# An attention and MLP kernel: the last row tile of the output in column parts of 384 and 128

## The chip, the cores and the metric

The kernel runs on one core of a Trainium2 chip. The metric is the device time of one execution in microseconds. The core has TensorE (PE) for matmuls, with a queue of weight loads of its own (PEld), VectorE (DVE), ScalarE (ACT), GpSimd (POOL) and SyncE (SP), which issues DMA transfers here. PE writes its results to PSUM, in tiles of 128 partitions by up to 512 f32 columns.

## The reference

Two things are computed one after the other. First, attention with a choice of key chunks, for 4 batches, 8 heads, 768 positions and a head size of 64; then a layer norm and a two-layer MLP with a residual, over rows of 512 (8 heads by 64):

```python
# attention, per batch and head: 24 chunks of 32 keys, 6 chosen for each query
ub = sum(max(q * k_min, q * k_max), -1)          # per query and chunk
top_chunks = argsort(where(causal, ub, -1e9))[..., -6:]
scores = q @ k.T / sqrt(64)
attn = softmax(where(chosen & causal, scores, -1e9))
x = (attn @ v)                                    # -> [4, 768, 512]
# MLP
xn = (x - mean) / sqrt(var + 1e-6) * g_ln
out = x + maximum(xn @ w_ch1, 0) @ w_ch2          # w_ch1 [512, 2048], w_ch2 [2048, 512]
```

## The kernel before

A unit of attention is `g`: one batch and one pair of heads, 16 in all. A half `r` is three row tiles of 128 positions (`TR` = 3), so a batch has two halves. For a unit, `load_qk` and `load_v` fetch its inputs, `turn` transposes them on PE, `k_bound` (DVE) and `k_copy` (ACT) read the transposed keys from one PSUM tile `tr`, `q_copy`, `q_ring` and `mask_ring` fill operand buffers, `bounds` and `select` choose the chunks, `scores` computes scores and their exponentials, `diag` (POOL) clears what lies above the diagonal, and `values` and `normalise` make `x`.

For a half of a batch, `stats`, `centre`, `x_t` and `rstd` do the norm. `mlp1(b, r, m)` computes two of the 16 blocks of the hidden layer: 8 matmuls of 384 columns (line 512) and one ReLU on ACT into `hT` (line 516). `mlp2(b, r, i, j)` computes a quarter of the contraction for row tile `i`: four matmuls of 512 columns (line 524) that add to one PSUM tile `yp`. After the quarter `j` = 3, DVE scales `yp` by `rstd` and adds `x` into `ot` (line 530), and SP stores `ot` (line 535). The `ot` pool has two buffers.

`w1_load` and `w2_load` fetch the weights in quarters, on POOL's queue, as `load_v` does; each w2 quarter holds the rows that one `j` needs.

The order of the program is written as a list of 894 pieces. A piece is one call of such a function, and it has a time, in units of one `g`, at which it should come. A table `MOVED` adds an offset to the time of a piece or of all pieces with the same first arguments (the longest matching key counts). The sorted list is the order in which the pieces are written. The pieces of the first part (`begin`, up to the norm of batch 0) are tied together in that order on each of PE, DVE, ACT and POOL. The others are placed by a scheduler that takes the list's order as priority, on each engine's queue, and it may let a ready piece go ahead of one that it thinks is waiting. Semaphores for all of it, PSUM tiles included, are made by the framework.

The last pieces of the list before the change are `mlp2(3, 1, 2, j)`, for the third row tile of the last half, in the order j = 0, 2, 1, 3.

Of the kernel before, what the change touches and what calls it, by code (L numbers as in the profile page):

```python
# [19 lines left out]
def kernel(  # L20
# [13 lines left out]
    nc = tc.nc  # L34
    P = nc.NUM_PARTITIONS

    B, H, S, D = q.shape
# [4 lines left out]
    NR = 2  # L42
    TR = NT // NR
# [4 lines left out]
    DM = H * D  # L48
    HID = moe_w_ch1.shape[1]
    KT1 = DM // P  # L50
    KT2 = HID // P
# [98 lines left out]
    w2b = const.tile([P, KT2, DM], F16, name="w2b", tag="w2b")  # L150
# [21 lines left out]
    def xh(b, r):  # L172
        if (b, r) not in x_tiles:
            x_tiles[b, r] = xp.tile([P, TR, H, D], F32, name="x", tag="x")
        return x_tiles[b, r]
# [215 lines left out]
    for r in range(NR):  # L391
        n = 0
# [125 lines left out]
    def mlp2(b, r, i, j):  # L518
        h = hf[b, r]
        if j == 0:  # L520
            h["yp"] = ps_t.tile([P, DM], F32, name="yp", tag="one")
        yp = h["yp"]
        for kt in range(4 * j, 4 * j + 4):
            nc.tensor.matmul(  # L524
                yp, h["hT"][:, kt, i * P:(i + 1) * P], w2b[:, kt, :],
                start=(kt == 0), stop=(kt == KT2 - 1),
            )
        if j == 3:
            ot = outp.tile([P, DM], F32, name="ot", tag="ot")
            nc.vector.scalar_tensor_tensor(  # L530
                ot, yp, h["rstd"][:, i:i + 1], xh(b, r)[:, i].rearrange("p h d -> p (h d)"),
                op0=ALU.mult, op1=ALU.add,
            )
            s = TR * r + i
            nc.sync.dma_start(out[b, s * P:(s + 1) * P, :], ot)
# [34 lines left out]
    for n in range(-3, U + LAG + 1):  # L570
# [13 lines left out]
        if new:  # L584
            g, i = new
# [76 lines left out]
    for b in range(B):  # L662
        e = 4.0 * b + GAP
        for r in range(NR):
            f = e + (-0.56 if r == 0 else 0.0)
            if b > 0:
                for i in range(TR):
                    at(f, stats, b, r, i)
                for i in range(TR):
                    at(f, centre, b, r, i)  # L670
                for kt in range(KT1):
                    at(f + 0.01, x_t, b, r, kt)
            at(f + 0.2 if b > 0 else ready[r], rstd, b, r)
        e += 0.06
        z = 4.0 * (b + 1) + GAP + 0.06
        m = (e + z) / 2
        if b == 0:
            spread(mlp1, b, 0, ready[0], -1.0)
            spread(mlp2, b, 0, -1.0, e)
            spread(mlp1, b, 1, e, m)  # L680
            spread(mlp2, b, 1, m, z)
            continue
        spread(mlp1, b, 0, e, m)
        spread(mlp1, b, 1, m, z)
        spread(mlp2, b, 0, m + 0.01, z)
        spread(mlp2, b, 1, z + 0.01, z + 2.0)
# [5 lines left out]
            (2,): 0, (2, 4): 0.006, (2, 5): 0.028, (3,): 0, (3, 1): 0.013, (3, 2): 0.013,  # L692
            (4,): -0.048, (5,): 0.008, (5, 5): 0.016, (6,): 0.004, (7,): -0.067, (7, 1): -0.07,
            (8,): -0.436, (9,): -0.025, (9, 5): -0.02, (11,): -0.044, (12,): -0.311, (13,): -0.144,
            (14,): -0.138, (14, 5): -0.134, (15,): -0.21, (15, 4): -0.176, (15, 5): 0,
        },
        "centre": {
            (): 0.008, (0,): -0.017, (0, 1): 0, (0, 1, 0): -0.017, (1,): 0, (1, 0, 2): 0.089,
            (1, 1): 0.033, (1, 1, 1): 0.026,
# [3 lines left out]
            (3, 0): -0.003, (3, 1): 0, (4,): -0.056, (6, 0): -0.044, (6, 1): -0.066, (7, 0): -0.178,  # L703
            (7, 1): -0.097, (8, 0): -0.399, (8, 1): -0.6, (9, 0): -0.066, (9, 1): -0.069, (11, 0): 0,
            (11, 1): -0.054, (12, 0): -0.04, (12, 1): 0, (13, 0): -0.146, (13, 1): -0.078,
            (14, 0): 0.003, (14, 1): 0, (15, 0): -0.621,
# [8 lines left out]
            (0,): -0.004, (1, 0): 0.161, (1, 1): 0.063, (2,): 0.006, (3, 0): -0.011, (3, 1): 0.054,  # L715
            (4,): 0.024, (5, 0): 0.511, (5, 1): 0.42, (6,): 0.038, (7, 0): -0.032, (9, 1): 0.023,
            (10,): 0.034, (11, 1): 0.026, (12, 0): 0.938, (12, 1): 0.253, (13, 0): 0.002,
            (13, 1): 0.073, (14,): 0.046, (15,): 0.034,
        },
        "k_diag": {  # L720
            (1,): 0.041, (2, 0): 0.13, (3, 0): 0.033, (3, 1): 0.01, (4,): -0.002, (6,): 0.002,
# [12 lines left out]
            (2,): -0.087, (3, 0): -0.13, (3, 1): -0.568, (4,): -0.551, (5,): -0.547, (6,): -0.163,  # L734
            (7,): 0.215, (8,): -0.124, (9,): 0.342, (12,): 0.279, (13,): 0.241, (14,): 0.301,
            (15,): 0.238,
        },
        "mask_ring": {
            (): 0.017, (0, 0): 0.021, (0, 1): 0, (1, 0): 0.036, (1, 1): -0.009, (2, 0): 0.023,
            (2, 1): 0, (4,): 0.064, (5,): 0.074, (6,): 0.076, (7,): 0.016, (8,): -0.257, (9,): 0.076,  # L740
# [5 lines left out]
            (13,): -0.082, (14,): 0, (15,): -0.006,  # L746
        },
        "mlp1": {
            (0, 0, 2): -0.016, (0, 0, 6): 0.106, (0, 0, 10): 0.098, (0, 0, 14): 0.069,
            (0, 1): -0.023, (0, 1, 0): 0, (0, 1, 2): 0.016, (0, 1, 14): 0.055, (1,): -0.026,  # L750
            (1, 0, 0): 0.016, (1, 0, 2): 0.016, (1, 0, 4): 0.028, (1, 0, 8): -0.014,
            (1, 1, 0): -0.036, (1, 1, 4): -0.178, (1, 1, 10): 0, (1, 1, 14): -0.001, (2,): -0.294,
            (2, 0, 6): -0.616, (2, 0, 12): -0.277, (2, 1, 2): -0.353, (2, 1, 6): -0.28,
            (2, 1, 10): -0.228, (3,): 0.103, (3, 0, 2): 0, (3, 0, 4): 0, (3, 0, 12): 0,
            (3, 0, 14): 0, (3, 1, 0): 0, (3, 1, 4): 0.108, (3, 1, 6): 0, (3, 1, 14): 0.094,
        },
        "mlp2": {
            (): -0.156, (0, 0, 1, 0): -0.071, (0, 0, 1, 3): 0, (0, 0, 2, 0): -0.051, (0, 1): -0.154,
# [5 lines left out]
            (2, 0, 2, 3): -0.34, (2, 1): 0, (2, 1, 0, 0): -0.34, (2, 1, 0, 1): -0.18,  # L764
            (2, 1, 0, 2): -0.323, (2, 1, 0, 3): -0.298, (2, 1, 1, 0): -0.267, (2, 1, 1, 1): -0.298,
            (2, 1, 1, 2): -0.423, (2, 1, 1, 3): -0.568, (3,): -0.233, (3, 0, 0): 0,
            (3, 0, 0, 2): -0.124, (3, 0, 0, 3): -0.233, (3, 0, 2): -0.332, (3, 1, 0, 0): -0.332,
            (3, 1, 0, 1): -0.374, (3, 1, 1, 1): -0.263, (3, 1, 1, 2): -0.443, (3, 1, 1, 3): -0.009,
            (3, 1, 2, 0): -0.009, (3, 1, 2, 1): 0.115, (3, 1, 2, 2): -0.224, (3, 1, 2, 3): -0.152,
        },  # L770
        "normalise": {
            (1, 0): -0.008, (2,): 0.002, (3,): -0.004, (4, 0): -0.01, (4, 1): -0.002, (6,): 0.002,
            (7,): -0.058, (8,): -0.331, (9,): 0.002, (12,): 0.006, (13,): -0.032, (14, 0): 0.065,
            (14, 1): 0.028,
# [4 lines left out]
            (11,): -0.002, (12, 0): 0, (12, 1): 0.16, (13,): -0.026, (14, 0): 0.066, (14, 1): 0.028,  # L779
        },  # L780
        "q_copy": {
            (): 0.051, (0,): 0.005, (1, 0): 0.005, (1, 1): 0, (2, 0): 0.007, (2, 1): 0, (3,): -0.012,
# [6 lines left out]
            (11,): 0.063, (12,): -0.045, (13,): 0.022,  # L789
# [3 lines left out]
            (10,): 0.167, (11,): 0, (12,): 0.141, (13,): 0.114, (14,): 0.096,  # L793
# [5 lines left out]
            (0,): -0.015, (0, 0, 0): -0.007, (0, 0, 1): 0.015, (1,): 0.018, (1, 1): 0.002,  # L799
            (1, 1, 2): 0.059, (1, 1, 3): 0.047, (2,): 0.038, (2, 1): 0.023, (2, 1, 0): -0.014,  # L800
            (2, 1, 1): 0.021, (3,): 0.017, (3, 0): 0.016, (4,): 0.001, (4, 1, 3): 0, (5, 1): -0.013,
            (5, 1, 0): 0, (6,): -0.144, (6, 1, 1): -0.087, (6, 1, 2): -0.133, (6, 1, 3): -0.092,
            (7,): -0.134, (7, 0, 0): -0.079, (7, 1, 0): -0.114, (7, 1, 2): -0.18, (8,): -0.582,
            (8, 0, 0): -0.504, (8, 0, 1): -0.612, (9,): -0.011, (9, 1): 0.013, (9, 1, 0): -0.011,
            (10,): -0.013, (10, 1, 2): -0.017, (10, 1, 3): -0.017, (11, 0, 0): 0.047,
            (11, 0, 1): 0.051, (11, 1, 0): -0.103, (11, 1, 1): -0.006, (11, 1, 2): 0.113,
            (11, 1, 3): 0.065, (12, 1, 2): -0.128, (12, 1, 3): -0.007, (13,): -0.028,
            (13, 0, 0): -0.042, (13, 1, 2): -0.062, (13, 1, 3): -0.042, (14,): 0.015,
            (14, 1, 3): 0.138, (15,): -0.31, (15, 1, 0): -0.355,
        },  # L810
        "select": {
            (1, 1): 0.01, (2, 0): -0.003, (2, 1): 0.002, (3, 0): -0.004, (3, 1): 0.048, (4,): 0.059,
            (5,): 0.335, (6,): 0.013, (7,): -0.056, (8,): -0.234, (9,): 0.454, (11,): -0.008,
            (12,): 0.17, (13,): -0.024, (14,): 0.028, (15,): 0.025,
# [19 lines left out]
            (): 0.027, (2,): 0.029, (3,): 0,  # L834
        },
        "x_t": {
            (): 0.474, (0,): 0.003, (0, 0, 0): 0, (0, 0, 3): 0.004, (0, 1, 1): -0.012,
            (1, 0, 0): 0.324, (2,): 0.123, (2, 0, 3): 0.242, (2, 1): 0.24, (2, 1, 3): 0.286,
            (3,): 0.695, (3, 1, 2): 0.739, (3, 1, 3): 0.529,
# [12 lines left out]
    for _, _, fn, args, kept in sorted(pieces, key=lambda x: x[:2]):  # L852
        done = nc.cur_bb.bb.instructions
        n = len(done)
# [36 lines left out]
```

## Time and profile before

| | |
|---|---|
| median of 7 runs | 303.09 us (302.03 to 303.98) |
| the profiled execution, its own time | 303.68 us |
| its span in the profile | 301.4 us |
| TensorE clock granted, mean | 0.999 |
| matmuls (PE) busy | 288.3 us |
| line 524, second MLP layer | 384 matmuls, 95.9 us busy, 379 ns each |
| line 530, the add on DVE | 24, 17.9 us, 745 ns each |
| line 535, stores of the output | 24 of 256 KB, median 2.2 us from issue to landing |

The span is the time from the first to the last instruction of the profile; the execution's own time is longer by what lies around it. In a row of a group, the numbers after the bar are the busy time in microseconds and the mean duration of one instruction in nanoseconds, then the idle time of the engine just before and what ended it. Matmuls are pipelined: their durations overlap, so the distance between the starts of two matmuls is what a sum needs. In the timeline the columns are start, length, engine, line, operation, and in brackets the idle time before it.

### The profile page before, as it was taken

What the parts mean: (1) busy time and instruction counts of PE and PEld (TensorE: products, weight loads), DVE (VectorE), ACT (ScalarE), POOL (GpSimd) and SP (SyncE); (2) the same over time, 40 slices, a digit from 0 to 9 for tenths busy, and PEclk for the clock granted to TensorE, in tenths of its full rate; (3) what the DMA queues carried; (4) which work ended last, traced back from release to release, by engine and by line L of the source; (5) the groups of instructions that cost most, each with busy time, mean ns of one, the idle gap of its engine ahead of it and who ended that gap; (6) DMA issues with size and microseconds to landing.
All of it is one profiled execution on the core that took longest, in us unless ns stands there. A gap on an engine that the chain in (4) does not pass through costs nothing.

```text
span 301.4 us, 7194 instructions
## 1 busy us (share of the span) xinstructions
PE 288.3 (96%) x2753; PEld 195.7 (65%) x2753; DVE 190.9 (63%) x654; ACT 183.4 (61%) x274; POOL 91.2 (30%) x162
## 2 busy tenths in 40 slices
PE   7887998999999999999999999999999999999993
PEld 3874766765777676777767667666666555555541
DVE  7888655679998788999577768577262282011011
ACT  3983998664788667778665674848368524423310
POOL 9559383152444412733230411223021120000000
PEclk9999999999999999999999999999999999999999
DMA  7999999999659659579482210113010110010111
GB/s 131 210 201 211 180 193 196 163 200 187 165 127 178 124 84 165 106 143 151 88 133 61 77 47 2 41 49 90 35 37 0 37 37 35 35 37 35 70 37 71
DMA packets 90226, 31.41 MB, mean 104 GB/s; under 512 B 78416, under 2 KB 87120, under 8 KB 90192
## 3 DMA queue, kind: packets, MB, share of 16 engines
q1 hardware_dynamic: 60416, 23.61, 34.2%
q0 software_dynamic: 29248, 7.34, 24.9%
q8 instruction: 22, 0.36, 0.5%
q14 instruction: 12, 0.10, 0.1%
q10 hardware_dynamic: 528, 0.00, 0.1%
HBM read 27.27 MB, written 6.29 MB: 111 GB/s over the span
## 4 chain that ended last, share of the span: by engine, by line
PE 75%; DMA 8%; POOL 7%; issue 4%; DVE 4%; ACT 1%; POOLq 0%; ACTq 0%
PE yp L524 24%; PE mm L512 24%; PE mm L411 10%; PE sm L437 6%; PE tr L223 4%; DMA w2b<-in_moe_w_ch_dram 4%; DMA w1b<-in_moe_w_ch_dram 4%; PE ub L326 3%; POOL va L214 2%; PE trh L497 1%; POOL pt L424 1%; PE trh L354 1%; DVE xc L482 1%; ACT pt L417 1%; POOL rstd L491 1%
## 5 line engine op out<-in xcount | busy, mean ns | idle before, releaser
L417 ACT ACTIVATE pt<-mm 128x1024 f16<-128x1024 f32 (+1 forms) x96 | 86.2, 918 | 25.7 <-PE mm L411 25.3
L524 PE MATMUL yp<-w2b,hT 128*128 128x512 f16 x384 | 95.9, 379 | 1.5 <-DMA w2b<-in_moe_w_ch_dram 1.5
L512 PE MATMUL mm<-xT,w1b 128*128 128x384 f16 x512 | 94.3, 326 | 0.0
L516 ACT ACTIVATE hT<-mm 128x768 f16<-128x768 f32 x64 | 51.9, 813 | 49.1 <-PE mm L512 48.8
L512 PEld LDWEIGHTS <-w1b 128*128 128x128 f16 x512 | 48.9, 98 | 29.9 <-issue 0.2
L524 PEld LDWEIGHTS <-hT 128*128 128x128 f16 x384 | 36.3, 98 | 31.8
L424 POOL TENSOR_SCALAR_AFFINE_SELECT pt<-pt 128x768 f16<-128x768 f16 x32 | 28.8, 899 | 89.2 <-ACT pt L417 89.2
L530 DVE SCALAR_TENSOR_TENSOR ot<-yp,rstd,x 128x512 f32<-128x512 f32 x24 | 17.9, 745 | 46.0 <-PE yp L524 46.0
L411 PE MATMUL mm<-QA,KA 128*128 128x128 f16 (+2 forms) x224 | 34.5, 245 | 1.0 <-ACT hT L516 0.5
L411 PE MATMUL mm<-QB,KB 128*128 128x128 f16 (+2 forms) x224 | 34.2, 246 | 0.0
L437 PEld LDWEIGHTS <-pt 128*128 128x128 f16 x672 | 24.6, 98 | 5.6 <-POOL pt L424 1.8
L437 PE MATMUL sm<-va,pt 128*128 128x65 f16 x672 | 26.5, 193 | 1.4 <-POOL pt L424 1.3
L411 PEld LDWEIGHTS <-KA 128*128 128x128 f16 x224 | 17.9, 99 | 8.1 <-issue 2.3
L471 DVE BATCH_NORM_STATS2 bst<-x 128x6 f32<-128x128 f32 x96 | 21.9, 281 | 0.8
L268 DVE TENSOR_REDUCE kc<-tr 128x12 f32<-128x384 f32 x32 | 17.5, 548 | 6.6 <-PE tr L223 4.9
L411 PEld LDWEIGHTS <-KB 128*128 128x128 f16 x224 | 17.9, 98 | 3.5 <-issue 0.8
L446 DVE RECIPROCAL rden<-sm 128x6 f32<-128x6 f32 x32 | 6.1, 191 | 19.7 <-PE sm L437 19.5
L447 DVE TENSOR_TENSOR x<-sm,rden 128x384 f32<-128x384 f32 x32 | 17.8, 556 | 1.0
L269 DVE TENSOR_REDUCE kc<-tr 128x12 f32<-128x384 f32 x32 | 17.5, 546 | 0.0
L223 PE MATMUL tr<-ident_f,qn 128*128 128x128 f32 x96 | 16.4, 281 | 1.0 <-DMA qn<-in_q_dram 0.8
L279 ACT CAST kh<-tr 128x384 f16<-128x384 f32 x24 | 11.6, 484 | 9.2 <-DVE kc L269 5.0
L223 PE MATMUL tr<-ident_f,kn 128*128 128x128 f32 x96 | 16.5, 283 | 0.0
(87 smaller groups left out, 354.6 us busy)
## 6 DMA issues: line engine op xcount, KB each, us to landing
kn<-in_k_dram SPq DMA_DIRECT2D x64, 96.0 KB, 3.4
qn<-in_q_dram SPq DMA_DIRECT2D x64, 96.0 KB, 3.8
out_dram<-ot SPq DMA_DIRECT2D x24, 256.0 KB, 2.2
va<-in_v_dram POOLq DMA_DIRECT2D x12, 192.0 KB, 5.8
w1b<-in_moe_w_ch_dram POOLq DMA_DIRECT2D x4, 512.0 KB, 8.2
w2b<-in_moe_w_ch_dram POOLq DMA_DIRECT2D x4, 512.0 KB, 11.1
KA<-kh SPq DMA_DIRECT2D x24, 48.0 KB, 2.4
KB<-kh SPq DMA_DIRECT2D x24, 48.0 KB, 2.0
```

What stands on the lines that cost most here:

```text
L223: nc.tensor.transpose(pst[:, t * P:(t + 1) * P], src[:, t], ident_f)
L268: nc.vector.tensor_reduce(kc[:, 0, n], view, axis=AX.X, op=ALU.min)
L411: nc.tensor.matmul(sc[:, hh, o:o + w * P], ks[:, t * P:(t + 1) * P], qs[:, s * P:(s + w) * P], start=True, stop=True,)
L417: nc.scalar.activation(pt[:, n0:n1].rearrange("p n h x -> p h n x"), sc[:, :, 0:o].rearrange("p h (n x) -> p h n x", x=P), ACTF.Exp, scale ...
L424: nc.gpsimd.affine_select(out=dv, in_=dv, compare_op=ALU.is_ge, fill=0.0, base=0, pattern=[[0, 2 * TR], [1, P]], channel_multiplier=-1,)
L437: nc.tensor.matmul(pv[:, hh, s2, :], pt[:, where[t, s], hh, :], va[:, hh, t, 0:D + 1], start=(t == 0), stop=(t == s),)
L447: nc.vector.tensor_tensor(xh(b, r)[:, :, 2 * hp:2 * hp + 2, :].rearrange("p s h d -> p h s d"), pv[:, :, :, 0:D], rden.to_broadcast([P, 2, ...
L471: nc.vector.bn_stats(h["st"][:, i, hp], xh(b, r)[:, i, 2 * hp:2 * hp + 2].rearrange("p h d -> p (h d)"),)
L512: nc.tensor.matmul(hp_[:, i, 0:TR * P], w1b[:, kt, (m + i) * P:(m + i + 1) * P], h["xT"][:, kt], start=(kt == 0), stop=(kt == KT1 - 1),)
L516: nc.scalar.activation(h["hT"][:, m:m + 2], hp_[:, :, 0:TR * P], ACTF.Relu, scale=HS)
L524: nc.tensor.matmul(yp, h["hT"][:, kt, i * P:(i + 1) * P], w2b[:, kt, :], start=(kt == 0), stop=(kt == KT2 - 1),)
L530: nc.vector.scalar_tensor_tensor(ot, yp, h["rstd"][:, i:i + 1], xh(b, r)[:, i].rearrange("p h d -> p (h d)"), op0=ALU.mult, op1=ALU.add,)
```

## The change

The last row tile of the output (batch 3, half 1, tile 2) is computed in two column parts. Its pieces j = 0 and 1 multiply the whole contraction, eight steps each, for columns 0 to 383; j = 2 and 3 do the same for columns 384 to 511. Each part is added and stored after its own last matmul, into a new `ot` buffer. Both parts use the one PSUM tile `yp`. All other row tiles are computed as before.

In the table, 66 pieces that had an offset of zero get one, and the four pieces of this row tile, which had offsets, have none, so that their order is 0, 1, 2, 3. All other offsets stay.

```diff
-        for kt in range(4 * j, 4 * j + 4):
+
+        n, cs = 4, slice(0, DM)
+        if (b, r, i) == (B - 1, NR - 1, TR - 1):
+            n, cs = 8, slice(0, DM - P) if j < 2 else slice(DM - P, DM)
+        for kt in range(n * j % KT2, n * j % KT2 + n):
             nc.tensor.matmul(
-                yp, h["hT"][:, kt, i * P:(i + 1) * P], w2b[:, kt, :],
+                yp[:, cs], h["hT"][:, kt, i * P:(i + 1) * P], w2b[:, kt, cs],
                 start=(kt == 0), stop=(kt == KT2 - 1),
             )
-        if j == 3:
+        if kt == KT2 - 1:
             ot = outp.tile([P, DM], F32, name="ot", tag="ot")
             nc.vector.scalar_tensor_tensor(
-                ot, yp, h["rstd"][:, i:i + 1], xh(b, r)[:, i].rearrange("p h d -> p (h d)"),
+                ot[:, cs], yp[:, cs], h["rstd"][:, i:i + 1], xh(b, r)[:, i].rearrange("p h d -> p (h d)")[:, cs],
                 op0=ALU.mult, op1=ALU.add,
             )
             s = TR * r + i
-            nc.sync.dma_start(out[b, s * P:(s + 1) * P, :], ot)
+            nc.sync.dma_start(out[b, s * P:(s + 1) * P, cs], ot[:, cs])
```

In the table, the pieces whose place in time changes most are these (offset in units of one `g`, before and after):

| piece | before | after |
|---|---|---|
| load_v(0, 0), (1, 0), (1, 1) | 0 | -0.126 |
| load_v(0, 1) | 0 | -0.08 |
| w1_load(3, 3) | 0 | 0.023 |
| w2_load(0, 0), (1, 0), (2, 1), (3, 1) | 0 | 0.047, 0.035, -0.032, -0.038 |
| k_diag(2, 1); mask_ring(2, 1) | 0 | 0.13; 0.136 |
| mlp2(0, 0, 1, 3) | 0 | -0.156 |
| k_copy(8, 0), (8, 1) | 0 | -0.141, -0.216 |
| load_v(10), (11) | 0 | 0.5, 0.265 |
| q_ring(11) | 0 | 1.082 |
| pair_stats(12, 0) | 0 | 0.16 |
| diag(12, 1) | 0 | -0.108 |
| bounds(15, 5) | 0 | -0.21 |
| mlp1(3, 0, 2), (3, 0, 4), (3, 0, 12), (3, 0, 14), (3, 1, 0) | 0 | 0.103 |
| mlp2(2, 1, 2, 0) to (2, 1, 2, 3) | 0 | -0.423 |
| mlp2(3, 0, 0, 0), (3, 0, 0, 1) | 0 | -0.233 |
| mlp2(3, 1, 2, 0), (.., 1), (.., 2), (.., 3) | -0.009, 0.115, -0.224, -0.152 | 0 |

The rest of the 66 moves by less than 0.11 each: single pieces of q_copy, k_copy, bounds, select, mask_t, mask_ring, scores, diag, normalise, pair_stats, centre, x_t, q_relu and mlp1.

## The prediction

> **What bounds the kernel now.** I read the page first, for the engine that limits and for the chain of waits.
>
> ```profile
> PE 288.3 (96%) x2753; PEld 195.7 (65%) x2753; DVE 190.9 (63%) x654; ACT 183.4 (61%) x274; POOL 91.2 (30%) x162
> ...
> PE 75%; DMA 8%; POOL 7%; issue 4%; DVE 4%; ACT 1%; POOLq 0%; ACTq 0%
> ```
>
> TensorE works in 96% of the span, and three quarters of the chain that ended last are its matmuls. The windows view (columns PE, PEld, DVE, ACT, POOL, clock, DMA) tells where it is dense:
>
> ```profile
> 0.00:54.00 54.00, 46.45 (x419) 34.88 (x420) 38.27 (x148) 40.23 (x76) 33.79 (x63) 1.00 1.25 189
> 54.00:100.00 46.00, 45.31 (x511) 33.25 (x510) 40.08 (x135) 33.54 (x50) 17.10 (x31) 1.00 1.10 168
> 100.00:200.00 100.00, 99.72 (x1097) 71.07 (x1096) 78.12 (x270) 68.25 (x97) 31.73 (x56) 1.00 0.50 93
> 200.00:297.00 97.00, 96.86 (x735) 56.51 (x733) 33.75 (x104) 41.34 (x53) 8.60 (x12) 1.00 0.12 40
> ```
>
> From 54 to 297 us PE is idle for 243.00 - 241.89 = 1.1 us in all. Another order there can win no more than that, and loses only where it makes PE wait. Before 54 us PE is idle for 7.6 us; its timeline shows one large piece of that:
>
> ```profile
> 49.65 1.89 PE L524 MATMUL yp<-w2b,hT 128*128 128x512 f16 x8
> 53.00 0.38 PE L524 MATMUL yp<-w2b,hT 128*128 128x512 f16 x1 [1.46 <-DMA w2b<-in_moe_w_ch_dram]
> 53.21 0.33 PE L354 MATMUL trh<-ident_h,MN 128*128 128x128 f16 x3
> ```
>
> One matmul of mlp2(0,0,0,2) stands at the head of PE's queue until its quarter of w2b has landed. Then comes the end, which no matmul hides (timeline of the last stretch):
>
> ```profile
> 288.07 8.80 PE L524 MATMUL yp<-w2b,hT 128*128 128x512 f16 x40
> ...
> 296.90 0.75 DVE L530 SCALAR_TENSOR_TENSOR ot<-yp,rstd,x 128x512 f32<-128x512 f32 x1 [2.70 <-PE yp L524]
> ```
>
> The add runs from 296.90 to 297.65, its store is issued at 297.68, and the DMA view gives 2.0 us to landing there: 299.7. From there to the span's end, 301.4, are 1.7 us of closing waits and barriers, which the change leaves alone.
>
> **The tail, part by part.** Durations come from the groups by shape, spacings from the timeline (second fence).
>
> ```profile
> L530 DVE SCALAR_TENSOR_TENSOR ot<-yp,rstd,x 128x512 f32<-128x512 f32 x24 | 17.9, 745 | 46.0 <-PE yp L524 46.0
> L247 DVE SCALAR_TENSOR_TENSOR q<-tr,q 128x384 f16<-128x384 f32 x12 | 6.6, 546 | 3.6 <-ACT q L246 3.6
> L247 DVE SCALAR_TENSOR_TENSOR q<-tr,q 128x256 f16<-128x256 f32 x12 | 5.0, 416 | 3.3 <-ACT q L246 3.1
> ```
>
> ```profile
> 286.77 1.46 PE L512 MATMUL mm<-xT,w1b 128*128 128x384 f16 x8
> ```
>
> *Matmuls.* The 40 at the end start (8.80 - 0.379)/39 = 0.216 us apart, so the 16 of the last row tile begin at 288.07 + 24 x 0.216 = 293.25. Matmuls of 384 columns start (1.46 - 0.326)/7 = 0.162 apart; those of 128 columns (0.33 - 0.219)/2 = 0.055, from the three at 53.21. Removed: 16 x 0.216 = 3.46. Added: 16 x 0.162 + 16 x 0.055 = 3.47. The columns are the same, so this costs nothing. The 16 further weight loads (98 ns each) run beside matmuls: the 65-column ones of L437 also load weights each time, and 30 of them take 0.91 us in the chain.
>
> *The add.* L247 is the same operation: (546 - 416)/128 = 1.02 ns a column. From 745 ns at 512 columns this makes 0.615 us for 384 and 0.355 us for 128 (bounds: 0.282, a statistics instruction of 128 columns, and 0.416, the row of 256). Two adds last 0.97 instead of 0.75, but only the short one would be left after the last matmul, if the long one ran beside the right part's matmuls.
>
> *Whether it does.* Both parts lie in one PSUM tile, yp: 512 f32 columns. This kernel's trace shows what the program does when two engines use one such tile without needing each other's data. k_bound (DVE, L269) and k_copy (ACT, L279) both only read tr:
>
> ```profile
> 155.99 0.55 DVE L269 TENSOR_REDUCE kc<-tr 128x12 f32<-128x384 f32 x1
> 156.69 0.48 ACT L279 CAST kh<-tr 128x384 f16<-128x384 f32 x1 [0.69 <-DVE kc L269]
> ```
>
> ACT was idle for 0.69 us and started 0.15 us after the reduce ended; in the table of waits this pair stands with 5.0 us in 4 waits. So accesses to one tile are put in order even where both read. I take it that the right part's first matmul waits for the left part's add. It is the last work in PE's queue, so all 16 right matmuls, then the second add, the second store and the barrier stand behind that wait, and nothing else fills it. That row has two readers; PE writing beside a reader of other columns does not occur in this trace. The page "PSUM — Partial Sum Buffer" of the Trainium skill, section "PSUM bank collisions raise a hardware error", goes further than the row and speaks against the change: two engines must not use one 2 KiB bank in the same partitions at once, disjoint columns and a PE write beside a DVE read included. By the page the sum below is the only one; by the row alone, the overlapped sum (second rival) stays possible too.
>
> *Sum.* Last left matmul starts at 293.25 + 15 x 0.162 = 295.68 and ends 0.326 later, 296.01. The add follows 0.04 later (now 296.86 to 296.90): 296.05 to 296.66. PE restarts 0.06 to 0.15 later; I take 0.06, as x_t starts that long after its centre. Right: 296.72 + 15 x 0.055 + 0.22 = 297.77; add 297.81 to 298.16; store issued 298.19, which is 0.51 later than now.
>
> *The store.* The last one moves 64 KB instead of 256. Nearest rows: 256 KB in 2.0 us and 48 KB (KA<-kh, in the quiet stretch 160 to 170) in 1.8. In the end stretch the DMA engines were busy for about 0.8 us of the 2.0, from 298.5 to 299.3. A quarter of the data could save 0.7 of that, or nothing. I take 1.7, near the 48 KB row, whose issue takes longer; ends 1.3 and 2.0. The page "DMA: Bandwidth & Descriptors", section "Anatomy of one DMA — SWDGE (gpsimd) path", has a fixed 2.0 us plus bytes at 436 GB/s; by that the saving would be 0.45 us, but also 2.6 us for the 256 KB that take 2.0 here. The left store (192 KB) is issued at 296.7 and is gone before the right one. One DMA more on SP costs its 0.33 us of issue inside PE's second part.
>
> Landing: 298.19 + 1.7 = 299.9 against 299.7, so **+0.2 us**; ends -0.3 (short add, landing 1.3) and +0.7 (landing 2.0, slow restart, 256-column add).
>
> **The table.** I added the offsets up for all 894 pieces. 66 that had none get one, the four of the last row tile lose theirs, and about 35 places in the list change. Most pass pieces of other engines or of other queues (w2_load past k_diag, mlp1(1,1,10) past diag), which reorders no queue. Real changes: load_v(0,1) stands before both w1_loads in POOL's queue, two issues of 0.75 us each; in the w2b loads that follow, the same transfers remain ahead. Centre(0,1,2) passes half of k_bound(5,1) on DVE, up to 0.5 us earlier for x_t near 74 us. Q_ring(11) falls behind on SP, 20 us before its use. The four mlp2(2,1,2) and two mlp2(3,0,0) pass mlp1 pieces after 255 us, where PE does not wait at all. I take zero for all of it. Ends: the 1.5 us wait at 51.2 and the 1.1 us later could vanish (-2.6), or PE's queue could get a new wait like the one at 51.2 (+3.1, worked out below).
>
> **Sum.** The profiled execution took 303.68 with a span of 301.4; with +0.2 it is 303.9. It lies 0.6 above the median of the runs, 303.09, so against that **303.3**.
>
> **Rivals.** *Slower: a second early wait for w2b.* The chain shows where it would be:
>
> ```profile
> 40.79 12.16 DMA w2b<-in_moe_w_ch_dram
> ```
>
> The third quarter lands at 52.95; the fourth, issued 1.2 us later, takes 14.3 us (the longest of the four) and lands at 56.3. Matmuls of mlp2 are not held to the hand-written order of the first pieces, and one of them slipped in ahead of mask_t(2,1). If, with the new places, one of mlp2(0,0,0,3) also slips in ahead of work that is ready, PE stands until 56.3: up to 56.3 - 53.2 = 3.1 us, half of it typically, 1.5. It decides as soon as that matmul is queued more than 0.9 us of work too early. For it: this stretch holds most of the moved loads. Against: the hand-written order there hardly changes. It gives 303.3 + 1.5 = **304.8**. Smaller new waits of PE on ACT, between 85 and 125 us, count here too.
>
> *Overlapped tail.* If the adds overlap, the right matmuls end at 296.9, the second add runs 296.93 to 297.29 and its store lands at 299.0: -0.7, **302.4**. Against it stands the order between k_bound and k_copy.
>
> *Faster.* The same early matmul goes behind mask_t(2,1), whose input was ready near 51.4: the 1.5 us wait vanishes, **301.8**. Against: the transfers ahead of w2b are the same, so it lands no earlier.
>
> **How the numbers follow.** About 0.3% (0.9 us) is what a measurement of this kernel can tell from no change. Serial tail and neutral places 0.38 (302.8 to 303.8); overlapped tail 0.05; both within 0.3%, 0.43 together. New waits 0.35, slower; waits gone 0.22, faster. The range reaches to both, 302.0 to 304.9; below and above it I leave about a tenth each. The likeliest case alone has 302.8 to 303.8.
>
> **What would show it.** Right: 16 matmuls of 384 columns from about 4 us before the end of PE, a hole of 0.7 us on PE that ends with DVE L530, 16 of 128 columns, adds near 0.61 and 0.36 us, a last store of 64 KB in 1.3 to 2.0 us, and 1.5 us of waiting for w2b as now. Wrong: no hole before the right matmuls (overlap); a w2b wait that is gone or doubled; PE idle by more than 1.1 us between 54 us and the last row tile.

## The result, and the profile after

| | before | after |
|---|---|---|
| median of the runs | 303.15 us (71 runs) | 301.76 us (28 runs) |
| ratio, with its 95% interval | | 0.9944 [0.9929, 0.9959] |
| the profiled execution, its own time | 303.68 us | 301.32 us |
| its span | 301.4 us | 299.4 us |

The kernel became faster by 0.56% by the ratio (0.41 to 0.71%) and by 1.4 us, 0.46%, by the medians. The forecast was 303.3, with a range from 302.0 to 304.9. The page gives the same picture of the bound as before, with 16 matmuls more:

```profile
PE 287.8 (96%) x2769; PEld 196.0 (65%) x2769; DVE 190.5 (64%) x655; ACT 182.9 (61%) x274; POOL 90.8 (30%) x162
...
PE 79%; DVE 9%; ACT 6%; DMA 2%; SPq 2%; issue 1%; POOL 0%; ACTq 0%
```

In the second line, the chain that ended last, DMA fell from 8% to 2% and POOL from 7% to nothing. So some transfer that used to be in the chain is no longer there. The windows view (PE, PEld, DVE, ACT, POOL, clock, DMA, GB/s) tells in which stretch:

```profile
0.00:54.00 54.00, 47.38 (x433) 35.61 (x434) 39.54 (x153) 41.92 (x78) 33.85 (x63) 1.00 1.27 189
54.00:100.00 46.00, 45.60 (x536) 33.57 (x534) 38.87 (x130) 33.65 (x50) 18.18 (x36) 1.00 1.06 169
100.00:200.00 100.00, 99.54 (x1099) 70.88 (x1096) 79.31 (x281) 66.40 (x96) 30.11 (x52) 1.00 0.49 93
```

In the first 54 us PE does 14 matmuls more than before (433 against 419) and is idle 0.9 us less. Between 54 and 100 it gains 0.3 us, and between 100 and 200 it loses 0.2. The end of the first stretch, in PE's timeline:

```profile
49.16 2.15 PE L528 MATMUL yp<-w2b,hT 128*128 128x512 f16 x9
51.15 0.33 PE L354 MATMUL trh<-ident_h,MN 128*128 128x128 f16 x3
```

Before, the ninth of these matmuls stood 1.46 us at the head of PE's queue, and mask_t came at 53.21. Now all nine run in one row and mask_t comes at 51.15. The matmul is still ahead of mask_t; its data comes sooner. The third quarter of w2b lands at 50.89 us instead of 52.95. The row also starts 0.49 us earlier (49.16 against 49.65), so 1.6 of the 2.06 us by which mask_t comes sooner are the wait. The reason shows on POOL, which issues it. POOL's timeline before (in brackets, the idle time before the instruction and what ended it):

```profile
26.02 4.64 POOL L214 DMA_DIRECT2D va<-in_v_dram  x6
33.01 0.76 POOL L214 DMA_DIRECT2D va<-in_v_dram  x1 [2.35 <-DMA w1b<-in_moe_w_ch_dram]
36.15 0.77 POOL L214 DMA_DIRECT2D va<-in_v_dram  x1 [2.38 <-DMA w1b<-in_moe_w_ch_dram]
...
40.79 0.75 POOL L166 DMA_DIRECT2D w2b<-in_moe_w_ch_dram  x1 [0.30 <-POOL w2b L165]
```

And after:

```profile
27.30 4.58 POOL L214 DMA_DIRECT2D va<-in_v_dram  x6
...
33.45 0.82 POOL L166 DMA_DIRECT2D w2b<-in_moe_w_ch_dram  x1 [0.51 <-POOL w2b L165]
...
36.40 0.75 POOL L166 DMA_DIRECT2D w2b<-in_moe_w_ch_dram  x1 [1.94 <-DMA w1b<-in_moe_w_ch_dram]
...
37.61 0.75 POOL L166 DMA_DIRECT2D w2b<-in_moe_w_ch_dram  x1 [0.30 <-POOL w2b L165]
```

Count the issues from the third quarter of w1, in the order of issue. Before, it is followed by the fourth and by eight of `load_v`; the seventh and the eighth of these, each eight issues behind a w1 quarter, do not start until that quarter has landed, at 32.72 and 35.86. The records of the traces name the reason. A semaphore is a counter by which an engine learns that a transfer has landed. In this program POOL's transfers use eight of them in turn (111 to 118), and an issue first waits for the transfer that had its semaphore before. The last two w1 quarters have 113 and 114, and so have the seventh and the eighth `load_v`. POOL stands 4.7 us in those two waits, and everything behind them stands too: `rstd` and all four quarters of w2b.

After the change, the two issues of load_v(0,1) come before these w1 quarters. The six that remain behind them run through, and the first two w2b issues are now eight behind (semaphores 115 and 116, as the two w1 quarters). The w1 quarters land at nearly the same times (32.92 and 35.86), but w2b is now what waits for them, and no longer what stands behind those that wait; POOL is idle ahead of these two issues for 0.51 and 1.94 us, of which 0.30 stands ahead of the other two as well. The w2b quarters are issued at 33.45, 36.40, 37.61 and 38.83 instead of 38.27, 39.57, 40.79 and 42.01.

The tail, in the timeline of the end:

```profile
294.30 0.62 DVE L534 SCALAR_TENSOR_TENSOR ot<-yp,rstd,x 128x384 f32<-128x384 f32 x1 [1.85 <-PE yp L528]
294.97 1.05 PE L528 MATMUL yp<-w2b,hT 128*128 128x128 f16 x16 [0.71 <-DVE ot L534]
...
296.06 0.35 DVE L534 SCALAR_TENSOR_TENSOR ot<-yp,rstd,x 128x128 f32<-128x128 f32 x1 [1.14 <-PE yp L528]
```

PE has its hole of 0.71 us, ended by the left add. The last store is issued at 296.44 and lands at 298.10. From the first matmul of the last row tile (293.25 before, 291.50 after) to the landing it is 6.47 us before and 6.60 after.

### The profile page after: what moved, and what is told of

The parts are those of the page before. It is cut to its first block, busy times and chain, and to the rows that moved or that the text cites. A ratio compares the mean times of both kernels' runs of the same rounds, so it can differ in the third digit from the quotient of the medians.

```text
span 299.4 us, 7230 instructions
## 1 busy us (share of the span) xinstructions
PE 287.8 (96%) x2769; PEld 196.0 (65%) x2769; DVE 190.5 (64%) x655; ACT 182.9 (61%) x274; POOL 90.8 (30%) x162
## 4 chain that ended last, share of the span: by engine, by line
PE 79%; DVE 9%; ACT 6%; DMA 2%; SPq 2%; issue 1%; POOL 0%; ACTq 0%
PE yp L528 26%; PE mm L512 24%; PE mm L411 11%; PE sm L437 6%; PE tr L223 5%; PE ub L326 3%; DMA qn<-in_q_dram 2%; SPq L195 2%; ACT hT L516 2%; DVE xc L482 2%; PE trh L497 1%; PE trh L354 1%; PE ub L316 1%; DVE bst L471 1%; DVE x L447 1%
## 5 line engine op out<-in xcount | busy, mean ns | idle before, releaser
L528 PE MATMUL yp<-w2b,hT 128*128 128x512 f16 (+2 forms) x400 | 96.5, 370 | 0.7 <-DVE ot L534 0.7
L528 PEld LDWEIGHTS <-hT 128*128 128x128 f16 x400 | 37.3, 98 | 31.5 <-issue 0.9
L534 DVE SCALAR_TENSOR_TENSOR ot<-yp,rstd,x 128x512 f32<-128x512 f32 (+2 forms) x25 | 18.1, 725 | 46.5 <-PE yp L528 46.0
L501 ACT ACTIVATE xT<-trh,gstr 128x384 f16<-128x384 f16 x16 | 8.8, 581 | 12.7 <-PE trh L497 12.6
L223 PE MATMUL tr<-ident_f,kn 128*128 128x128 f32 x96 | 15.9, 275 | 0.3 <-DMA kn<-in_k_dram 0.2
```

Of the source, the lines that this page charges most:

```text
L223: nc.tensor.transpose(pst[:, t * P:(t + 1) * P], src[:, t], ident_f)
L528: nc.tensor.matmul(yp[:, cs], h["hT"][:, kt, i * P:(i + 1) * P], w2b[:, kt, cs], start=(kt == 0), stop=(kt == KT2 - 1),)
L534: nc.vector.scalar_tensor_tensor(ot[:, cs], yp[:, cs], h["rstd"][:, i:i + 1], xh(b, r)[:, i].rearrange("p h d -> p (h d)")[:, cs], op0=ALU ...
```

## The experiments

The theory after the traces (A): load_v(0,1) ahead of the last w1 quarters lets w2b be issued earlier, and this is nearly all of the gain. Its rival (B): the other new places, the tail, or the start of the program make it. In the four series of runs below the kernel before had medians of 303.13, 303.20, 303.08 and 303.26 us. All times are medians; the profiles give the place.

**One part at a time.** e1_tail is the kernel before with the change to `mlp2` alone, and zero offsets for the four pieces of the last row tile. e2_places is the kernel before with the new table alone, those four pieces left at their old offsets. e3_v01 is the kernel before with one new place:

```diff
+    MOVED["load_v"][0, 1] = -0.08
```

e1_tail: 

> The column parts alone: the last row tile as in the changed kernel, its four offsets zero, every other offset as before. On every engine the order is that of before up to the last row tile. Theory 'early loads' (the gain comes from w2b landing earlier): PE still waits 1.5 us for w2b near 51 us and everything up to the last row tile is as before; from the first matmul of the last row tile to the end of the span 7.9 us instead of 8.2, as in the changed kernel's trace (landing 0.1 later, closing waits 0.4 shorter). Time 0.0 to 0.4 us below before. Rival 'tail' (the parts bring the gain): 1.2 us or more below before.

e2_places: 

> The new offsets alone: all 66 pieces moved as in the changed kernel, the last row tile computed whole, with its old offsets. Theory 'early loads': 1.2 to 1.8 us below before, the wait for w2b near 51 us gone, the third quarter of w2b landed near 51 instead of 53. Rival 'tail': within 0.4 us of before.

e3_v01: 

> One offset alone: load_v(0,1) at -0.08, all else as before. Only POOL's queue differs: the two issues of load_v(0,1) stand before the last two w1 quarters instead of behind them. Theory 'early loads': third quarter of w2b lands near 51, PE's wait of 1.5 us for it is gone or under 0.3, everything after it 1.5 to 2.0 us earlier, time 1.2 to 2.0 below before. Rival 'many places' (the gain is spread over the other 65 moved pieces): within 0.4 us of before. My own prediction had priced this move at zero, because the same transfers remain ahead of w2b.

Measured: e1_tail 303.38, ratio 1.0009 [0.9985, 1.0033]; e2_places 302.55, 0.9977 [0.9954, 1.0001]; e3_v01 302.65, 0.9990 [0.9960, 1.0021]. The third quarter of w2b landed at 52.21, 51.53 and 52.00 us. The direction fits A, but e2_places and e3_v01 are 0.6 and 0.5 us below before where A expected 1.2 or more, the intervals of all three reach to no change, and tail and table together would make 302.8 (0.25 more and 0.58 less than the 303.13 of before), not the changed kernel's time. So two were run again:

e1_again: 

> The kernel before with only the last rows in parts, a second time. By the profile's rows (landing 0.13 us later, closing 0.4 us shorter, 0.2 us more outside the span): 303.0 to 303.2 us, no difference. If the first median holds: 303.4.

e3_again: 

> The kernel before with only load_v(0,1) ahead of w1, a second time. Its first median, 302.65, has four of twelve runs at a granted clock under 0.995; the other eight have 302.0. If the place is worth about 1 us: 302.0 to 302.3. If it is worth half: 302.6.

e1_again has 302.90, 0.9989 [0.9974, 1.0004], e3_again 302.29, 0.9964 [0.9935, 0.9992]. Both repeats thus lie 0.4 to 0.5 us below the first run of the same kernel. Of all 24 runs of each, the median is 303.18 for the tail (no difference from before) and 302.38 for load_v(0,1), 0.8 us below before.

**Taking load_v(0,1) back, and building the two parts up.** e6_no_v01 is the changed kernel with

```diff
+    MOVED["load_v"][0, 1] = 0
```

and e8_v01_tail is e1_tail with the line of e3_v01. The changed kernel ran beside them.

a1_after: 

> The changed kernel again, beside the three kernels that take something from it or build it up. Both theories: 301.8 us, 0.993 to 0.997 of the kernel before; the third quarter of w2b lands near 51 us and PE does not wait 1.46 us for it.

e6_no_v01: 

> The changed kernel with the two loads of mask 1's v in the first row (load_v(0,1)) put back behind both halves of w1. Theory A (these two loads, moved into a gap of POOL's queue, bring w2b forward and so end PE's wait): the third quarter of w2b lands at 52.2 to 52.9 us, PE waits 0.8 to 1.5 us for it, and the time is 0.8 to 1.5 us above the changed kernel. Theory B (the gain comes from the other new places or from the start): third quarter and time stay within 0.3 us of the changed kernel.

e8_v01_tail: 

> The kernel before with only two parts of the change: load_v(0,1) ahead of w1, and the last rows in parts of 384 and 128. Theory A: these two are the whole change, 301.8 us and a third quarter of w2b at 51.0 us. If the other places do a share of it: between 302.3 and 302.9, third quarter 51.5 to 52.0. If the parts only add up as measured one by one (load_v(0,1) 0.999, tail 1.0009): 303.1.

a1_after 302.34, 0.9963 [0.9932, 0.9994]; e6_no_v01 302.85, 0.9978 [0.9953, 1.0003]; e8_v01_tail 302.02, 0.9955 [0.9932, 0.9978]. With load_v(0,1) back at its old place the wait is there again, shorter than in the profile of before (PE's timeline of e6_no_v01):

```profile
52.32 0.38 PE L528 MATMUL yp<-w2b,hT 128*128 128x512 f16 x1 [0.82 <-DMA w2b<-in_moe_w_ch_dram]
52.54 0.33 PE L354 MATMUL trh<-ident_h,MN 128*128 128x128 f16 x3
```

mask_t comes 0.97 us after that of a1_after (51.57), and the time rises by 0.5. Theory A expected 0.8 to 1.5, theory B 0.3 at most; the two intervals overlap, so the trace decides here, not the time. And e8_v01_tail, with two parts of the change and no other new place, has the changed kernel's time. Its one profile is not a typical one: with a time of 303.08, a us above its own median, it shows a landing at 52.51, because there the two w1 quarters landed over a us later than in the profile of after (34.21 and 37.58).

**The order of the transfers or the time of the issue.** The prediction had said that the transfers ahead of w2b stay the same. In truth two of them go earlier *and* the issue of w2b goes earlier. e5_held keeps the first and takes the second away, by holding POOL ahead of the first w2b issue:

```diff
+        _ = [nc.gpsimd.memset(held, 0.0) for _ in range(6)] if j == 0 else 0
         nc.gpsimd.tensor_copy(w2b[0:1, 4 * j, 0:1], st[g]["kc"][0:1, 0, NCH // 2:NCH // 2 + 1])
```

> The changed kernel with POOL held by six memsets just before it issues the first quarter of w2b, so that w2b is issued near 38 us as before the change, while the loads ahead of it keep their new places. Theory A1 (the queue has fewer bytes ahead of w2b): the third quarter still lands at 50.9 to 51.5 us and the time is within 0.4 us of the changed kernel. Theory A2 (the earlier issue itself brings w2b forward): it lands near 52.9, PE waits about 1.4 us, the time is 1 to 1.5 us above the changed kernel.

303.04 us, 0.9980 [0.9953, 1.0007], 0.7 above a1_after. POOL's timeline of e5_held:

```profile
33.00 4.72 POOL L165 MEMSET held<- 128x768 f16 x6
...
38.17 0.82 POOL L166 DMA_DIRECT2D w2b<-in_moe_w_ch_dram  x1 [0.30 <-POOL w2b L165]
```

The third quarter lands at 52.36 and PE waits 1.12 us:

```profile
52.40 0.38 PE L528 MATMUL yp<-w2b,hT 128*128 128x512 f16 x1 [1.12 <-DMA w2b<-in_moe_w_ch_dram]
```

So the order of the transfers alone brings little; the time of the issue decides (A2, though smaller than expected there). What the queue does meanwhile stands in the DMA view, from 34 to 42 us (packets, MB, share). e5_held:

```profile
q0 software_dynamic: 2758, 0.65, 83.0%
```

and the changed kernel:

```profile
q0 software_dynamic: 2979, 0.87, 99.4%
```

The kernel before moved 0.59 MB on this queue there, e6_no_v01 0.54, a1_after 0.84. While POOL stands, the queue has only what was issued to it earlier, and w2b's 512 KB quarters come late into it.

One measure is nearly free of the differences between executions: the time from the landing of the fourth w1 quarter, for which POOL waits in both orders, to the issue and the landing of the third w2b quarter. All the profiles of this study give it (us):

| load_v(0,1) | profiles | issue | landing |
|---|---|---|---|
| behind w1: before, e1_tail, e1_again, e6_no_v01, e11_pool6 | 5 | 4.9 to 5.1 | 16.9 to 17.1 |
| ahead of w1, POOL held: e5_held | 1 | 4.2 | 15.9 |
| ahead of w1: all others | 12 | 1.75 | 14.7 to 15.2 |

So the move is worth 2 us behind the w1 quarter. Some 1.2 us of it is given back ahead of that quarter, which is issued 1.1 to 1.9 us later and lands at 35.9 to 37.6 us (median 36.6) instead of 35.2 to 35.9 (35.4), leaving out e11_pool6, where it was issued 2 us late. With POOL held, what is left of the 2 us is no more than that, so what pays is the earlier issue. The median landing of the third w2b quarter is 51.6 us in the twelve profiles and 52.4 in the four others without e11_pool6: 0.8 us, which is what load_v(0,1) alone brought over 24 runs. The 2.06 us between the profiles of before and after are more, because there the fourth w1 quarter landed at 35.86 in both, though issued 1.26 us later in the second. And PE's wait for w2b is not always gone: in the twelve profiles the ninth matmul comes 0.0 to 1.1 us after its turn, in the four 0.8 to 1.6.

**A PSUM tile of its own for the right part.** e7_bank is the changed kernel with

```diff
-        if j == 0:
+        if j == 0 or (j == 2 and (b, r, i) == (B - 1, NR - 1, TR - 1)):
             h["yp"] = ps_t.tile([P, DM], F32, name="yp", tag="one")
```

e7_bank: 

> The changed kernel, with a second PSUM tile for the right column part; nothing else differs, the order on every engine is the same. Theory 'one tile is in order': the hole of 0.71 us before the right matmuls is gone, the long add runs beside them, the last store is issued 0.8 us earlier and lands 0.8 earlier; time 0.6 to 0.9 below the changed kernel, so 2.0 to 2.6 below before. Rival 'the stores queue up': the left store's 192 KB are still moving when the right store is issued, and only 0.3 to 0.5 of it is gained.

e7_again: 

> The changed kernel with a PSUM tile of its own for the last 128 columns, a second time, beside the two kernels built on it. 301.2 us as at first, 0.991 to 0.995 of the kernel before; no hole on PE before the right matmuls.

301.22, 0.9931 [0.9905, 0.9958], and 300.90, 0.9928 [0.9903, 0.9952]. The end of e7_bank's timeline:

```profile
286.47 8.84 PE L528 MATMUL yp<-w2b,hT 128*128 128x512 f16 x56
...
294.45 0.62 DVE L534 SCALAR_TENSOR_TENSOR ot<-yp,rstd,x 128x384 f32<-128x384 f32 x1 [1.85 <-PE yp L528]
295.35 0.35 DVE L534 SCALAR_TENSOR_TENSOR ot<-yp,rstd,x 128x128 f32<-128x128 f32 x1 [0.28 <-PE yp L528]
```

All 56 matmuls stand in one row; the 16 of the right part run beside the left add. From the first matmul of the last row tile to the landing it is 5.77 us instead of 6.60, and 6.47 before the change. The second PSUM tile is worth 0.8 us against the change as it is, and the column parts with it 0.7 against the whole row tile. This is the overlapped tail of the prediction, which said -0.7; it needs this edit, not the change as it is. The times agree (0.5 to 1.4 us below the changed kernel's 301.76 and 302.34), but those ran in other series. The stores do not queue up: the right one lands 1.69 us after its issue, though the left one lands only at 296.99. The Trainium skill, page "PSUM — Partial Sum Buffer", section "PSUM bank collisions raise a hardware error", lets two engines work at the same time in different banks, and this run agrees: PE writes one tile while DVE reads the other, with no hole between.

**What the rest of the table costs.** From the landing of the third quarter to the first matmul of the last row tile it is 240.1 to 240.3 us in the eight profiles of kernels with the old places (load_v(0,1) moved or not), and 240.5 to 241.2 in the nine of kernels with the new table. So the new places lose some 0.4 us on the way; e5_held is one of the nine (240.5), so holding POOL cost nothing further on. PE has two waits between 118 and 130 us in the changed kernel that the kernel before does not have, at 122.6 (0.19 us) and 128.8 (0.32 us), by the distance between the starts of neighbouring matmuls. e9_centre is e7_bank with one of its places undone, and e10_v01_bank has the old table:

```diff
+    MOVED["centre"][1, 0] = 0                # e9_centre: e7_bank with this
+    MOVED["load_v"][0, 1] = -0.08            # e10_v01_bank: e1_tail with this and e7_bank's PSUM tile
```

e9_centre: 

> The previous kernel with one of the new places undone: centre(1,0) stands again ahead of k_bound on DVE near 118 us. Theory C (this place costs what the changed kernel loses between 118 and 130 us): PE's waits of 0.19 and 0.32 us near 122.8 and 129.3 us are gone, and the time is 0.3 to 0.6 us below the previous kernel, near 300.8. Rival (other places there cost it): both waits stay, the time is within 0.15 us of the previous kernel.

e10_v01_bank: 

> The kernel before with load_v(0,1) ahead of w1 and the last rows in parts with a PSUM tile of their own each, all other places as before. If load_v(0,1) is the only new place that brings w2b forward: as the two kernels above or up to 0.4 us below the first of them, 300.8 to 301.3. If other new places share in it: 301.6 to 302.0.

e9_centre 300.61 (6 runs), 0.9912 [0.9881, 0.9943]; e10_v01_bank 301.36, 0.9937 [0.9911, 0.9962]. DVE in e7_bank, where `k_bound` goes ahead of `centre`:

```profile
118.08 0.54 DVE L269 TENSOR_REDUCE kc<-tr 128x12 f32<-128x384 f32 x1
118.54 1.48 DVE L482 TENSOR_SCALAR xc<-x,mv 128x512 f16<-128x512 f32 x2
120.05 0.47 DVE L482 TENSOR_SCALAR xc<-x,mv 128x512 f16<-128x512 f32 x1
```

and in e9_centre:

```profile
118.26 0.81 DVE L482 TENSOR_SCALAR xc<-x,mv 128x512 f16<-128x512 f32 x2
118.98 0.55 DVE L268 TENSOR_REDUCE kc<-tr 128x12 f32<-128x384 f32 x1
119.45 0.55 DVE L269 TENSOR_REDUCE kc<-tr 128x12 f32<-128x384 f32 x1
120.09 0.56 DVE L482 TENSOR_SCALAR xc<-x,mv 128x512 f16<-128x512 f32 x1
```

The two waits are gone, and the stretch after the landing is the shortest of all, 239.98 us. In the time it is 0.3 us less than e7_again; the intervals overlap, so the trace shows this step and the times only agree. e9_centre is the fastest kernel of the study, 2.5 us below before. e10_v01_bank has the time of e7_bank within their spread (301.36; 301.22 and 300.90): apart from load_v(0,1), the 65 other new places bring nothing that the times can tell.

**The edges of the program.** Two terms of the gain lie in no stretch of the work. From the landing of the last store to the span's end it is 1.70 us before and 1.29 after, and the time outside the span is 2.2 us before and 1.9 after. All other kernels with the last rows in parts close in 1.29 or 1.30, but for e5_held (1.58); e2_places and e3_v01, with the last rows in one, in 1.69. Outside the span, the medians are 2.36 to 2.38 in e1_tail, e8_v01_tail and e10_v01_bank, 2.2 in e3_v01 and e3_again, 1.90 to 1.94 in all kernels with the new table but e5_held (1.72). Three kernels add idle instructions: six memsets on POOL to the kernel before (e11_pool6), one memset on POOL (e12_pool1) or two small copies on ACT (e13_act2) to the changed kernel, written as

```diff
+        if (b, r, i, j) == (3, 0, 0, 0):
+            _ = [nc.gpsimd.memset(held, 0.0) for _ in range(6)]
```

e11_pool6: 

> The kernel before with six memsets of 8 columns on POOL near 240 us, where POOL is idle. Theory N (the number of instructions of an engine sets the times at the edges): time outside the span 1.9 to 2.1 instead of 2.2 us, or the closing away from 1.70 by 0.2 us or more; the time as before within 0.3 us. Rival (the order of the work sets them): 2.2 and 1.70 us as before.

e12_pool1: 

> The changed kernel with one memset more on POOL near 240 us: 195 instructions there, as before the change. Theory N with POOL: time outside the span 2.2 to 2.4 us instead of 1.90, 302.2 us. Rival: 1.90 us and 301.8 to 302.3.

e13_act2: 

> The changed kernel with two small copies more on ACT near 240 us: 366 instructions there, as before the change. Theory N with ACT: time outside the span 2.2 to 2.4 us instead of 1.90. Rival: 1.90 us.

The added instructions ran at 11 us (POOL) and 3.3 us (ACT), not near 240. e11_pool6: 303.12, 1.0007 [0.9980, 1.0035], outside the span 1.89, closing 2.13 in its one profile. e12_pool1: 302.21, 0.9955 [0.9925, 0.9985], outside 2.04. e13_act2: 302.38, 0.9986 [0.9966, 1.0006], outside 1.92. e11_pool6 has what theory N said for it; e12_pool1 and e13_act2 fell short of the 2.2 to 2.4 that it said for them. Of these additions only POOL's moved the edges, by 0.1 to 0.4 us, and e1_tail has as many instructions on POOL and ACT as the kernel before and yet closes in 1.29. So the count alone does not set them. What sets these edges stays open.

## Why the prediction was wrong

*What bounds.* Right: PE, dense from 54 us on, and the 1.46 us before mask_t (from 51.54, not from 51.2) as the one large piece that another order could win. The part of the gain that could be traced came from that piece.

*The tail.* The price of the tail was right step by step. Matmul columns cost nothing; the hole is 0.71 us (0.7 said); the adds last 0.62 and 0.35; the last store takes 1.66 us (1.7 taken); from the last row tile's first matmul to the landing it is 0.13 us more (0.2 said). The step "1.7 us of closing waits and barriers, which the change leaves alone" was wrong: 1.29, which is more than the tail lost. By the times, the tail alone makes no difference (303.18 over 24 runs).

*The table.* This is the step that failed, in one sentence: "load_v(0,1) stands before both w1_loads in POOL's queue, two issues of 0.75 us each; in the w2b loads that follow, the same transfers remain ahead." The move was priced at nothing, because the transfers ahead of w2b are the same. So far that was right: with their new order but POOL held, the third quarter of w2b lands at 52.36 us, as in the profiles with the old order (median 52.4), and the time is that of before within 0.2 us. What the step left out is when w2b is issued. Eight `load_v` issues stood behind the w1 quarters, and the last two of them (by the list of pieces load_v(1,1), not load_v(0,1)) carried POOL's two waits for w1:

```profile
POOL va L214 <- DMA w1b<-in_moe_w_ch_dram: 4.7, 2, 2.4
```

With two issues fewer behind w1, none of the rest meets these waits, and w2b no longer stands behind them. What moved was not 1.5 us of issue time but the place of the waits: the third quarter of w2b was issued 3.2 us earlier, counted from the landing of the w1 quarter, and landed 2 us earlier by that count and 0.8 us earlier in the median of the profiles. I had read the chain up to w2b's issue and had not asked what POOL waited for ahead of it. The list of real changes also lacks the swaps of the last two w1 quarters and of load_v(1,1) and (2,1). They are no part of the gain: e3_v01 does not have them, and its third quarter lands 15.05 us behind the w1 quarter all the same.

*The rival "Faster".* It gave 301.8 with the wait gone, and that is the time, but in part by luck. Its mechanism did not happen: no matmul went behind mask_t. The earlier w2b is worth some 0.8 us, and the rest lies in part at the edges of the program. The argument against it, "so it lands no earlier", was the failed step again, and it had put this case at 0.22. The prediction says that its range reaches to this case, but the range ends at 302.0.

*The rival "Slower".* No second matmul waited for w2b. But its smaller sibling, new waits of PE between 85 and 125 us, is there: 0.19 and 0.32 us, at 122.6 and just outside at 128.8, from centre(1,0) behind `k_bound`, so with DVE behind them and not ACT. Such waits were named, but not traced to that piece, which is not in the prediction's list of real changes.

*The sum.* By the experiments, load_v(0,1) is worth 0.5 us (taken out of the changed kernel), 0.8 (added alone) and 1.2 (added to the tail); the tail 0.0; the rest of the table between -0.3 and +0.3, its loss of 0.4 us on PE being set against 0.3 us less outside the span. These add up to about -0.8 to -1.2, against the measured -1.4. One kernel's medians differ by up to 0.6 us between two series (the changed kernel: 301.76 and 302.34), so the rest is not resolved.

## What to carry to other kernels

A DMA issue on an engine's queue can carry a wait for an earlier transfer, here the one eight issues ahead, and then the price of moving it is that wait for everything queued behind it, not the length of the issue. So before a moved load is priced at nothing, read what the issuing engine waits for, from the moved place up to the next load that the critical engine needs. Where executions differ, measure from an event that both orders wait for: here that gave the effect within 0.5 us where the landings themselves spread over 1.6. And two column parts of a last tile overlap only if the second has a PSUM tile of its own: here that is 0.8 us of a 6.6 us tail.

## What the runs showed of the hardware

- The landing of a queued transfer varies from execution to execution: the third quarter of w2b, with the same instructions ahead of it on POOL, landed at 50.89 and 51.31 us in two profiles of the changed kernel, at 51.53 in e2_places and at 52.51 in e8_v01_tail, and what follows shifts with it nearly one to one. Nearly all of this comes from the w1 quarter for which POOL waits, which landed at 35.86, 36.19, 36.53 and 37.58 in these four. A single profile of such a kernel is good for the mechanism, not for half a us.
- Smaller stores save little: 256 KB landed 2.04 us after issue, 192 KB in 1.87 and 64 KB in 1.66, about 0.4 us for 192 KB less. The Trainium skill, page "DMA: Bandwidth & Descriptors", section "Anatomy of one DMA — SWDGE (gpsimd) path", has 2.0 us plus bytes at 436 GB/s, for transfers that GpSimd issues; SP issues these stores. An estimate by that page is 2.6, 2.45 and 2.15 us; the slope nearly agrees (0.45 us for 192 KB), the fixed part is smaller here, 1.4 to 1.5.
- The time outside the span differs between programs whose work is nearly the same: 2.33 to 2.42 us over the 24 runs of the tail alone, 1.85 to 1.96 over the 12 of a1_after, 1.68 to 1.78 with POOL held. Half a us of a small gain or loss can lie there.
- PE starts slow for a time that varies, with the clock column at 1.00 throughout. The transposes from 4.74 us on start 0.21 us apart up to 6.4 us in the profile of before and up to 6.0 us in a1_after, but only up to 4.9 us in that of after, and 0.11 us apart from then on. The first nine matmuls on w2b start at 49.65, 49.55 and 49.16 us in these three, so up to 0.5 us of the lead of after's profile may come from the start and not from the change.
